# A new stored order for an attention and gated-MLP kernel: same instructions, other places and engines

## The chip, the cores and the metric

The kernel runs on one core of one Trainium2 chip. The metric is the device time of one execution in microseconds (us). PE is the matrix engine, DVE the vector engine, ACT the scalar engine, POOL the GpSimd engine, SP the sync engine, which here issues nearly all DMAs. Each of the five works through a queue of its own strictly in order and waits on semaphores where it needs another's result.

## The reference

Attention over 8 batches, 8 heads, 576 places, head size 64, with a bias that a small MLP makes from relative positions; its output goes through a gate (a causal convolution of 5 taps and a sigmoid), a product with w_val, and a product with w_out.

```python
scores = scale * np.matmul(q, k.transpose(0, 1, 3, 2))          # 8 x 8 x 576 x 576
x = (psi_rel / psi_i)[..., None]                                # log1p(|i-j|) / log1p(max(i,1))
bias = np.maximum(x @ w1 + b1, 0.0) @ w2                        # hidden 32, 8 heads
scores = scores + bias.transpose(2, 0, 1)[None]
attn = np.exp(scores - np.max(scores, axis=-1, keepdims=True))
attn = attn / (np.sum(attn, axis=-1, keepdims=True) + 1e-09)
x = np.matmul(attn, v)                                          # -> (8, 576, 512)
gate = sigmoid(sum_k conv_w[k] * shifted(x, k))                 # 5 taps
return gate * (x @ w_val) @ w_out
```

All is float32; the kernel splits the operands of the large products into a high and a low float16 part where it doesn't multiply in float32.

## The kernel before

**Start.** `bias_rows` makes the bias of 16 rows at a time: four `relu` tasks (L328 on ACT, L330 on DVE, or POOL), products on PE (L349), evictions (L368 on ACT, L370 on DVE), a store to DRAM by SP (L395). 36 such groups fill five tiles in DRAM, from which `load_bias` (L417, L420) loads the bias of a pair of heads, in the layout that the scores have.

**Attention.** `pair(n)` is one batch and two heads, 32 of them. SP loads its q and k (`qk_ld`, L610) into one of two `qk` buffers. Each pair has four blocks of 128 rows and half of a remainder block. A block is one QK product of 1.2 us on PE (L700, L716 for the remainder) into two `sp` tiles of PSUM, of which there are only two, so a block's two `logits` on DVE (L746: bias added, row maximum) must be over before the next QK product may start. Then come `expo` on ACT (L758), and one of two ways to transpose the weights. In 12 pairs ("T" in `TRANS`) the weights are normalised first (`norm`, L803) and PE transposes them (L848). In the other 20 they are split into float16 parts (`top`, L208 or L212 or L210; `rest`, L231, on POOL or DVE), and the DMA transposes them (`swap`, L882, L885, issued by SP). PE multiplies them with V (`piece`, L917) into a `po` tile, one of four PSUM tiles of the ring `ps`.

In the 20 pairs the sums are divided out afterwards, and here a `po` tile has two users beside the products: `ev` on ACT (L226) reads its first 256 columns, and `rb` on PE (L962) writes the broadcast reciprocals into its last 256, which `mu` on DVE (L972) reads. Neither needs the other's result, but they share the tile, and the one that comes later in the program waits for the one that comes first.

**MLP.** When a batch's four pairs are done, `mlp` makes its gate (convolution on DVE and ACT, L1097, L1106; tanh, L1118), the products `val` (L1172) and `outp` (L1227), and the stores. This work is spread between the QK products of later pairs.

**Preparation of weights.** `weight` takes each of nine weight pieces through six bit operations on DVE (`double_step`, L431 to L455) and a split. The absolute maximum of each V (`vmax`, L622, L635) is a DVE task too.

**What sets the order.** Every such step is a `Task` with the engines that may do it. `Plan.order` decodes a table, `ORDER`, of two bytes a task: the number of the task times four, plus which of its engines does it. The program is built in exactly that order; it gives each engine its queue, each tile its buffer from the ring, and decides which of two users of a tile comes first. Of 4115 tasks 1557 have more than one engine to choose from.

## Time and profile before

| | |
|---|---|
| median of 3 runs | 720.48 us (717.33 to 724.47) |
| the profiled execution | 725.42 us, its span 723.6 us |
| PE busy | 673.0 us |
| DVE busy | 639.4 us |
| ACT busy | 593.6 us |
| POOL busy | 446.5 us |
| granted TensorE clock, mean | 0.987 |

The page counts a matmul as busy from its start to its modelled end. A row of waits says which engine, line and tile waited, for what, and how long in total, how often, and at most. A row of the timeline is one instruction or a run of equal ones.

### The profile page before, as it was taken

How to read it: one execution, taken by the hardware profiler on the slowest of the kernel's cores; microseconds unless marked ns; L12 is line 12 of the kernel's file. 1: busy time of each engine (PE TensorE's matmuls, PEld its weight loads, DVE VectorE, ACT ScalarE, POOL GpSimd, SP SyncE). 2: the span in 40 equal slices, each digit the busy share in tenths (PEclk: the TensorE clock that was granted, in tenths of full speed). 3: DMA queues.
4: the chain of work that ended last, by engine and by line, in shares of the span. 5: the costliest groups of instructions: out<-in, count | busy, mean ns of one | idle time of the engine just before them, and what ended most of it. 6: DMA issues, size and time to landing. Idle time of an engine off the chain costs nothing. (4 is left out here: it accounts for less than half of the span.)

```text
span 723.6 us, 17323 instructions
## 1 busy us (share of the span) xinstructions
PE 673.0 (93%) x6144; PEld 421.0 (58%) x6144; DVE 639.4 (88%) x1656; ACT 593.6 (82%) x1323; POOL 446.5 (62%) x624
## 2 busy tenths in 40 slices
PE   6899899999999999888899999997999998998997
PEld 2225576666666755555567665564676665566754
DVE  7999799999998998997889898889889998888982
ACT  6999578988999987888668877798878898899761
POOL 0004455667788677667767778776658876766541
PEclk9999899999999999999999999998999999999999
DMA  5888972312299879999983589999953899899813
GB/s 161 262 311 294 318 234 63 125 67 62 70 158 180 193 171 199 220 222 185 175 184 97 127 176 199 202 210 199 190 125 99 181 209 189 177 201 202 150 45 116
DMA packets 263302, 125.73 MB, mean 174 GB/s; under 512 B 239792, under 2 KB 240048, under 8 KB 263216
## 3 DMA queue, kind: packets, MB, share of 16 engines
q1 hardware_dynamic: 263072, 124.34, 76.3%
q8 instruction: 48, 0.79, 0.5%
q10 hardware_dynamic: 144, 0.29, 0.1%
q14 instruction: 38, 0.31, 0.1%
HBM read 44.64 MB, written 20.33 MB: 90 GB/s over the span
## 5 line engine op out<-in xcount | busy, mean ns | idle before, releaser
L758 ACT ACTIVATE t_d<-t_d,nm 128x576 f32<-128x576 f32 x288 | 222.2, 774 | 45.1 <-DVE nm L746 39.4
L231 POOL TENSOR_TENSOR t_d<-t_d 128x512 f16<-128x512 f32 (+1 forms) x203 | 193.2, 969 | 71.6 <-ACT t_d L208 55.1
L746 DVE CUSTOM_DVE_ANT_0 t_d<-t_sp,bias 128x576 f32<-128x576 f32 x256 | 186.2, 749 | 25.2 <-PE t_sp L700 15.6
L700 PE MATMUL t_sp<-t_qk 64*128 64x288 f32 x1024 | 179.8, 433 | 9.9 <-DVE nm L746 7.4
L917 PE MATMUL t_ps<-t_pt,t_w 128*64 128x256 f16 (+1 forms) x1600 | 130.9, 309 | 8.1 <-DMA t_pt<-t_d 4.9
L700 PEld LDWEIGHTS t_sp<-t_qk 64*128 64x128 f32 x1024 | 101.6, 187 | 60.9 <-DVE nm L746 24.9
L803 POOL TENSOR_SCALAR t_d<-t_d,rinv 128x576 f32<-128x576 f32 x94 | 74.3, 801 | 43.6 <-DVE rinv L786 17.7
L208 ACT CAST t_d<-t_d 128x576 f16<-128x576 f32 x139 | 91.0, 667 | 8.0 <-DVE t_d L231 2.5
L1172 PEld LDWEIGHTS <-wv 128*128 128x128 f16 x768 | 72.7, 99 | 33.2 <-issue 11.9
L1172 PE MATMUL t_ps<-xh,wv 128*128 128x320 f16 (+1 forms) x512 | 75.9, 292 | 0.0
L848 PE MATMUL t_ps<-ident,t_d 128*128 128x128 f32 x486 | 69.9, 285 | 2.7 <-ACT t_pt L208 1.0
L917 PEld LDWEIGHTS <-t_w 128*64 128x64 f16 x1120 | 57.7, 110 | 25.2 <-issue 18.2
L848 PEld LDWEIGHTS t_ps<-ident,t_d 128*128 128x128 f32 x486 | 53.8, 143 | 25.9 <-issue 9.0
L1106 DVE SCALAR_TENSOR_TENSOR t_ps<-t_xp,convw,t_ps 128x288 f32<-128x288 f32 x126 | 65.2, 518 | 2.5 <-ACT t_ps L1097 0.3
L208 ACT COPY t_pt<-t_ps 128x512 f32<-128x512 f32 (+1 forms) x123 | 53.8, 480 | 11.3 <-PE t_ps L848 11.0
L1227 PE MATMUL t_ps<-wo,gh 128*128 128x512 f16 x256 | 61.7, 380 | 0.5 <-DVE gh L210 0.5
L758 ACT ACTIVATION_READ_ACCUMULATOR t_d<-t_d,nm 128x1 f32 x288 | 55.7, 194 | 0.0
L349 PE MATMUL t_ps<-rel,w 128*32 128x288 f32 (+17 forms) x352 | 46.1, 487 | 6.6 <-DVE rel L330 3.0
L231 DVE TENSOR_TENSOR t_d<-t_d 128x512 f16<-128x512 f32 (+1 forms) x67 | 48.5, 737 | 2.9 <-POOL t_d L212 1.5
L330 DVE TENSOR_SCALAR rel<-gt,sct,nb 128x576 f32<-128x576 f32 (+17 forms) x107 | 46.5, 500 | 0.0
L231 POOL TENSOR_TENSOR gl<-t_w,gh 128x256 f16<-128x256 f32 x42 | 29.3, 699 | 25.9 <-ACT gh L208 20.4
L917 PEld LDWEIGHTS t_ps<-t_pt,t_w 128*64 128x64 f32 x480 | 31.7, 137 | 23.1 <-issue 5.3
(139 smaller groups left out, 1078.8 us busy)
## 6 DMA issues: line engine op xcount, KB each, us to landing
t_qk<-qkd SPq DMA_DIRECT2D x32, 576.0 KB, 4.5
bias_d<-t_be SPq DMA_DIRECT2D x36, 295.5 KB, 6.0
bias<-bias_d SPq DMA_DIRECT2D x16, 576.0 KB, 7.1
out<-t_w SPq DMA_DIRECT2D x32, 256.0 KB, 2.6
t_w<-vd SPq DMA_DIRECT2D x20, 320.0 KB, 3.6
t_w<-vn SPq DMA_DIRECT2D x12, 320.0 KB, 3.7
t_d<-wvd SPq DMA_DIRECT2D x4, 512.0 KB, 5.1
t_d<-wod SPq DMA_DIRECT2D x4, 512.0 KB, 5.7
```

The lines of the kernel that those rows point to most:

```text
L208: A.copy(out=out, in_=in_)
L231: (V if e == "V" else G).tensor_tensor(out=out, in0=in0, in1=in1, op=ALU.subtract)
L330: (G if e == "G" else V).tensor_scalar(out=rel[g].t[:, 0:w], in0=src, scalar1=sct[:, mm : mm + 1], scalar2=nb1, op0=ALU.mult, op1=ALU.max,)
L700: T.matmul(ts[a][:, j, 0:hw], lhsT=qk.t[r, c * P : (c + 1) * P], rhs=qk.t[r, x : x + hw], start=True, stop=True,)
L746: V.tensor_tensor_reduce(out=part(c, a).rearrange("p (j f) -> p j f", j=2), in0=sp.t[:, :, 0 : S // 2], in1=bias.rearrange("p (j f) -> p j ...
L758: A.activation(out=part(c, a), in_=part(c, a), func=AF.Exp, bias=nms[c][:, a : a + 1], scale=-1.0, accum_out=sums[c][:, a, 0:1],)
L803: (G if e == "G" else V).tensor_scalar(out=t, in0=t, scalar1=rinvs[c][:, a : a + 1], scalar2=1.0, op0=ALU.mult, op1=ALU.mult,)
L848: T.transpose(t[:, k * P : (k + 1) * P], es[c].t[:, (k0 + k) * P : (k0 + k + 1) * P], ident)
L917: T.matmul(po.t[r, 0:256], lhsT=vt.t[:, v, r], rhs=pt[:, x, :, :] if tr else pt[:, :, x, :], start=(t == 0 and m == 0), stop=(t == 4 and m ...
L1106: V.scalar_tensor_tensor(out=o, in0=x, scalar=wt, in1=t, op0=ALU.mult, op1=ALU.add)
L1172: T.matmul(pm.t[:, 0:w], lhsT=weights["wv"][wi][:, k, d * P : (d + 1) * P], rhs=xb.t[xi][:, k, 0:w], start=(q == 0 and k == 0), stop=(q == ...
L1227: T.matmul(pm.t, lhsT=gb.t[gi][:, k, o : o + P] if o < 256 else gx.t[gi][:, k, :], rhs=weights["wo"][wi][:, k, :], start=(q == 0 and k == ...
```

## The change

Only `ORDER` is another. The tasks, what they depend on, the buffers and every other constant stand as before, and each engine's instructions come from the same tasks. 503 of the 1557 tasks with a choice go to another engine: 149 from DVE to POOL and 129 back, 71 from DVE to ACT and 63 back, 46 from POOL to ACT and 45 back. The number of PE instructions stays at 7637, and SP's at 286. In the new program the line numbers are lower by 2 than in the old one, as the table is two lines shorter: L700 becomes L698, L962 becomes L960.

The words that come with the change say that the table was searched for longer, with transfers taken to land later, and with the two users of a PSUM tile in sequence.

```diff
 BUFS = dict(w=13, d=6, pt=2, sp=2, ps=4, qk=2, rel=3, be=9, xp=2, xh=1, gh=1, gx=1)
 ORDER = (
-    'c-mE04`?Fyo}b+{W|EyGlQ?E4$s{`_lVr?Jl1VbzOp?jg9zL*#d$?c^d${0xxM0B^_OM_Nd)S8sd$?c^7cAJrJ>0_{?qR`qSg^%{3qG(9dswjG9`3^h7cAI^J?vrOzP~ZqzV{t}-{1H9`F_6N-'
...
+    'c-nPW0cav;n|60cGue!Bl8nhDnPex)BpJ<QGf5_!Nix}5u;35&a1RSE*ux$!_=7zxSg?l$d$@-M3+~~91s5#X!v+7t9`<m-9v1A6|6vac?qPo{Sg>Hhg8i{z!5;U1WA^WVaQEtb-'
...
 )
```

Three places show how queues change. The first is on PE, late in the program, at an `rb` (L962, later L960). The rows are PE's, with the semaphores that a row waits for; `wv` is w_val's float16 parts, `xl` the low part of the attention's output, `t_sp` the score tiles. Before:

```order
L1172 LDWEIGHTS wv_102
L1172 MATMUL t_ps<-xl,wv_102 128x320 [waits Pool_49]
L1172 LDWEIGHTS wv_102
L1172 MATMUL t_ps<-xl,wv_102 128x320
L962 MATMUL t_ps<-ident,rinvs 64x128 [waits Activation_49]
L962 MATMUL t_ps<-ident,rinvs 64x128 x3
L700 MATMUL t_sp<-t_qk 128x288 [waits DVE_49] x2
```

The same `rb` in the changed program; `t_pt` are transposed weights, `t_w` V:

```order
L915 LDWEIGHTS t_w
L915 MATMUL t_ps<-t_pt,t_w 64x256
L960 MATMUL t_ps<-ident,rinvs 64x128 x4
L698 MATMUL t_sp<-t_qk 128x288 [waits DMAHW6_49,DVE_49]
L698 MATMUL t_sp<-t_qk 128x288 [waits DVE_49]
L698 MATMUL t_sp<-t_qk 128x288 x2
```

The `rb` now follows its last `piece` at once and no longer waits for ACT: it stands ahead of `ev` in the table, so that `ev` waits for it. In the whole program ten rows of L962 wait for ACT before, and seven of L960 afterwards.

The second place is on PE too, where the program before has two QK products behind each other with nothing between (eight matmuls are two blocks); `gh` is the gated value's high part. Before:

```order
L1227 LDWEIGHTS gh
L1227 MATMUL t_ps<-wo_104,gh 128x512
L700 MATMUL t_sp<-t_qk 128x288 x8
L917 LDWEIGHTS t_w
L917 MATMUL t_ps<-t_pt,t_w 64x256
```

The first of these two QK blocks in the changed program:

```order
L1170 LDWEIGHTS wv_102
L1170 MATMUL t_ps<-xl,wv_102 128x320
L698 MATMUL t_sp<-t_qk 128x288 x4
L1170 LDWEIGHTS wv_102
L1170 MATMUL t_ps<-xh,wv_102 128x320
```

No two QK blocks stand together there any more: `val` products are on both sides.

The third is on DVE, in the start, among the `relu` rows (L330, later L328); `vcol` is V's maximum, `t_be` the bias rows, `t_w<-t_d` a step of the weight preparation. Before:

```order
L330 TENSOR_SCALAR rel<-gt,sct,nb_133 128x368 x3
L622 TENSOR_REDUCE vcol<-t_w 128x1
L330 TENSOR_SCALAR rel<-gt,sct,nb_133 128x336 x3
L330 TENSOR_SCALAR rel<-gt,sct,nb_133 128x352 x2
L370 TENSOR_SCALAR t_be<-t_ps,cadd 128x368
L330 TENSOR_SCALAR rel<-gt,sct,nb_133 128x352
L330 TENSOR_SCALAR rel<-gt,sct,nb_133 128x320 x3
L330 TENSOR_SCALAR rel<-gt,sct,nb_133 128x304
L622 TENSOR_REDUCE vcol<-t_w 128x1
```

The changed program at about the same rows:

```order
L328 TENSOR_SCALAR rel<-gt,sct,nb_133 128x400 x3
L328 TENSOR_SCALAR rel<-gt,sct,nb_133 128x384 x3
L429 TENSOR_SCALAR t_w<-t_d 128x512
L328 TENSOR_SCALAR rel<-gt,sct,nb_133 128x416 x3
L432 TENSOR_SCALAR t_w<-t_w 128x512
L328 TENSOR_SCALAR rel<-gt,sct,nb_133 128x352 x3
L328 TENSOR_SCALAR rel<-gt,sct,nb_133 128x368 x3
L328 TENSOR_SCALAR rel<-gt,sct,nb_133 128x304 x3
L435 TENSOR_SCALAR t_w<-t_w 128x512
```

Ahead of the last `relu` the old table has five `vmax`, seven `double_step` and four `logits` on DVE, the new one one, ten and six.

## The prediction

> **What bounds the kernel now.** I read the page's span and busy times first, then a table by stage, then the waits of PE, ACT and SP, and last single places in the timeline.

> ```profile
> span 723.6 us, 17323 instructions
> PE 673.0 (93%) x6144; PEld 421.0 (58%) x6144; DVE 639.4 (88%) x1656; ACT 593.6 (82%) x1323; POOL 446.5 (62%) x624
> 20.00:40.00 20.00, 17.59 (x131) 5.55 (x128) 19.97 (x51) 18.78 (x41) 1.43 (x1) 1.00 0.91 295
> 40.00:60.00 20.00, 18.51 (x132) 6.23 (x136) 20.00 (x50) 19.52 (x41) 0.00 (x0) 1.00 0.91 316
> 60.00:80.00 20.00, 15.01 (x118) 9.53 (x111) 16.83 (x48) 14.07 (x38) 10.16 (x13) 0.93 0.87 281
> 100.00:150.00 50.00, 49.24 (x431) 33.17 (x427) 48.69 (x142) 43.43 (x110) 32.27 (x47) 1.00 0.26 89
> 300.00:350.00 50.00, 43.63 (x461) 28.38 (x457) 44.18 (x110) 41.99 (x89) 36.22 (x43) 0.97 1.05 197
> 600.00:650.00 50.00, 46.33 (x433) 28.09 (x425) 43.26 (x107) 45.03 (x97) 33.61 (x44) 1.00 0.97 189
> 700.00:723.60 23.60, 19.17 (x105) 10.11 (x105) 8.55 (x18) 3.05 (x7) 6.16 (x13) 0.98 0.31 100
> ```

> The stages' columns are PE, its weight loads, DVE, ACT, POOL (busy us, instructions), granted clock, DMA share, GB/s. There are two regimes. From 20 to 60 us, while the bias is made, DVE has not 0.1 us free. From 100 us on PE is the busiest (49.24 of 50 us), but DVE follows closely (48.69), and in the loosest stretch PE has 6.4 us free (43.63 of 50). No PE instruction is added or removed, so the change can win only what PE, or DVE in the start, loses by waiting. If PE's busy time were its floor, that is 723.6 - 673.0 = 50.6 us at most.

> [...]

> What PE, ACT and SP wait for (total us, times, longest):

> ```profile
> PE t_sp L700 <- DVE nm L746: 7.4, 8, 3.4
> PE t_ps L962 <- ACT t_xp L226: 7.1, 5, 2.7
> PE t_ps L917 <- DMA t_pt<-t_d: 4.9, 6, 1.4
> PE t_ps L917 <- DMA t_w<-t_w: 2.5, 1, 2.5
> PE t_sp L700 <- DMA t_qk<-qkd: 2.0, 2, 1.3
> ACT t_xp L226 <- PE t_ps L962: 10.2, 9, 2.9
> SPq L610 <- PE t_sp L700: 51.4, 9, 12.0
> ```

> Two of the words that come with the change have a counterpart here: the two users of a PSUM tile (7.1 us of PE) and landings of DMAs (4.9 + 2.5 + 2.0 = 9.4 us).

> **The change part by part.** The sum is made against the profiled execution's 725.42 us, 0.7% above the median of 720.48; at the end the ratio is carried over to the median.

> *The two users of the tile.* The costliest case, PE's timeline (start, duration, wait in brackets):

> ```profile
> 602.89 1.25 PE L1172 MATMUL t_ps<-xh,wv 128*128 128x320 f16 x8
> 603.98 0.71 PE L1172 MATMUL t_ps<-xl,wv 128*128 128x320 f16 x4
> 607.42 0.66 PE L962 MATMUL t_ps<-ident,rinvs 128*64 128x128 f32 x8 [2.73 <-ACT t_xp L226]
> 608.01 1.24 PE L700 MATMUL t_sp<-t_qk 64*128 64x288 f32 x8
> ```

> This `rb` is the first place shown in the change: it waits 2.73 us for an ACT eviction whose result it doesn't need, and the QK product behind it waits too. Of the five `rb` that wait, four have lost their wait for ACT in the new table, this one among them; the fifth keeps it, but two `val` products now stand on PE in front. Seven rows still wait for ACT. If they cost nothing, 7.1 us go; if each costs the mean of the old ten (7.1 / 10 = 0.71), 7 x 0.71 = 5.0 stay and 2.1 go. By the table an `rb` comes after its `ev` 12 times before and 9 times afterwards; of the 12 six had no PE work at all between the two places, of the 9 one has none and the others 0.5 to 9 us. That is nearer to the first end. I take **-6.1 us**. What is late next: three more `ev` wait for `rb` instead (28 before, 31 now), at 10.2 / 28 = 0.36 us each, 1.1 us of ACT, which has 723.6 - 593.6 = 130 us free. I cost it at nothing; without that cover it is 1.1 us.

> *QK blocks that stand too close.* The second place of the change, in the trace of before:

> ```profile
> 282.76 1.95 PE L700 MATMUL t_sp<-t_qk 64*128 64x288 f32 x8
> 285.11 1.91 PE L700 MATMUL t_sp<-t_qk 64*128 64x288 f32 x8 [0.39 <-DVE nm L746]
> ```

> With nothing between them each block takes 0.7 us longer than the 1.24 us above, and 0.39 us of wait comes on top, because two score tiles must first be read by two `logits`. I added up the PE work that stands between one QK block and the next (taking, for instance, 1.25 / 2 us for four `val` matmuls as above), leaving out the start. Of 131 gaps 15 hold less than 1.5 us before, and 4 after; 5 hold more than 6 us before (the longest 10.7), and 1 after (6.6). Where a gap is long, DVE has no scores to read. So 11 places get rid of up to 0.7 us: -7.7 us at the most, and nothing if DVE, 88% busy, is late there anyhow. Between these ends I take about the middle, **-4 us**: the wait named after DVE above is 7.4 us in all, of which 3.4 us is a single one in the start.

> *The start.* DVE's prices there, and what moves between DVE and POOL (groups by shape):

> ```profile
> L622 DVE TENSOR_REDUCE vcol<-t_w 128x1 f32<-128x640 f32 x12 | 9.7, 809 | 0.0
> L437 DVE TENSOR_SCALAR t_w<-t_w 128x512 int32<-128x512 int32 (+1 forms) x9 | 3.7, 412 | 0.2
> L231 POOL TENSOR_TENSOR t_d<-t_d 128x512 f16<-128x512 f32 x132 | 158.3, 1206 | 69.6 <-ACT t_d L208 54.2 <-DVE t_w L1071 4.5 <-DVE t_d L210 3.6
> L231 DVE TENSOR_TENSOR t_d<-t_d 128x512 f16<-128x512 f32 x48 | 38.7, 809 | 2.9 <-POOL t_d L212 1.5 <-ACT t_d L208 1.1
> L231 POOL TENSOR_TENSOR gl<-t_w,gh 128x256 f16<-128x256 f32 x42 | 29.3, 699 | 25.9 <-ACT gh L208 20.4 <-ACT gxh L208 4.9 <-DVE gh L210 0.2
> ```

> Four `vmax` leave the full stretch of DVE (4 x 0.81 = 3.2 us) and three `double_step` enter it (3 x 0.41 = 1.2 us): 2.0 us less. The maxima return after 60 us, where DVE has 3.2 of 20 us free, so most of it holds. **-1.5 us**, between -3.2 and 0.

> *Subtractions that go to POOL.* Nine of 128x512 leave DVE: 9 x 0.809 = 7.3 us of DVE against 9 x 1.206 = 10.9 us of POOL, which has 277 us free. A single one is 0.4 us later on POOL. Were all nine on the path, that is +3.6 us; were DVE the bound throughout, -7.3. As neither is the busiest engine after 100 us I take **0**.

> [...]

> *Loads of q and k.* SP can issue such a load only when the buffer's old QK products are done, and PE's work from there to the first new QK product must cover the rest. The price is the landing, from issue, for L610:

> ```profile
> DMA to landing us min/median/max: 3.5/4.5/8.1
> ```

> Before, 4 of the 30 turns hold less than 7 us of PE work (4.8, 4.9, 6.2 and 6.3), and PE waited 2.0 us in two. Afterwards 8 do (five of 5.0 to 5.4, then 5.9, 6.6 and 6.7). Twice as many at the same price is **+2 us**. The lower end is 0; at the upper end all land after 8.1 us, a shortfall of 8 x 8.1 - 45.0 = 19.8 us against 4 x 8.1 - 22.2 = 10.2 before, so +9.6. The transposes by DMA (4.9 us) I leave as they are: the PE work between the place of a `swap` and its first `piece` has a median of 3.0 us before and 3.3 after.

> *The end.* Behind the last QK block PE's queue holds 4.5 us less work than before. PE's total is the same, so this is no term of its own.

> Sum: -6.1 - 4 - 1.5 + 0 + 2 = -9.6 us, 715.8 us for the profiled execution, a ratio of 0.987, and **711 us** for the median.

> **The rivals.** A measurement of this kernel tells a change of about 1% from none (713.3 to 727.7 us count as none; the three runs before lie 1% apart).

> *The waits move elsewhere.* DVE's load falls by 1% only, and a new order that frees PE of one wait meets another engine at 82 or 88%. Against it is that the waits named above had a direct cause in the order. With a net of -5 to +5 us the time is about 719.

> *The loads come late (slower).* Place: the first QK product of the pairs with the eight short turns; price: up to +9.6 us by themselves. SP must reach the load in its queue, in which L610 already stood up to 12.0 us behind PE's QK products, and the transposes stand behind it. It decides once SP is 2 us late on top of a landing of 4.5 us, since 5.0 to 5.4 us of cover are then gone: then each of the eight stalls PE by about 1.3 us, the longest of the two seen: 8 x 1.3 - 2.0 = +8.4 us. The transposes behind in SP's queue are late by as much, which doubles it, and half of the other gains is left: 720.5 + 16.8 - 5.8 = 731 us.

> [...]

> *A larger gain.* PE's busy time hides waits, as the 1.95 us show. If the QK gaps that are now even spare 0.15 us at each of 131 blocks, 20 us, twice the sum, go: 700 us.

> **How the numbers follow.** The forecast (-5 to -16 us) 0.50, of which 0.08 lies within 1%; the waits move 0.23; loads late 0.13; lock-out 0.04; larger gain 0.10. Faster by over 1%: 0.42 + 0.10 = 0.52. Within 1%: 0.08 + 0.21 + 0.04 = 0.33, and 0.02 of the moved waits with the late loads give 0.15 slower. The forecast's own range, 704 to 715, comes from the ends of its terms (-7.1 - 7.7 - 1.5 and -2.1 - 4 - 1.5 + 2). The range of all cases reaches to 725, which leaves out most of the late loads, and down to 700.

> **What would show it.** Right: the wait of L960 for ACT falls to about 1 us; L698 for DVE falls under 5 us; DVE at 20 to 60 us still full, but the first transposes on PE (L846) start 1 to 2 us earlier; PE's wait for t_qk at 4 us. Wrong: PE's busy time or its waits for t_qk, t_pt or DVE grow by more than these save. If L960's wait is gone and the time is the same, the waits have moved.

## The result and the profile after

The changed kernel takes 696.4 us (median of 4 runs, 692.2 to 698.7) against 720.7 us (the three runs of the table of before and one more): a ratio of 0.9655, 95% interval 0.9587 to 0.9722. Timed once more beside the experiments it gave 0.9616 (0.9581 to 0.9650). The forecast was 711 us, a ratio of 0.987, with a range of 700 to 725. The direction was right, the size was not, and the time fell below the range. The profiled execution took 698.68 us, its span is below.

Span, busy times and stages of the changed kernel, in the columns of the prediction:

```profile
span 696.2 us, 17319 instructions
PE 659.1 (95%) x6144; PEld 418.3 (60%) x6144; DVE 623.7 (90%) x1631; ACT 593.1 (85%) x1332; POOL 457.3 (66%) x637
20.00:40.00 20.00, 18.27 (x129) 5.57 (x126) 20.00 (x52) 19.51 (x43) 3.61 (x2) 1.00 0.99 337
40.00:60.00 20.00, 18.82 (x144) 6.78 (x147) 20.00 (x49) 18.90 (x42) 0.39 (x1) 1.00 0.96 313
60.00:80.00 20.00, 15.35 (x117) 8.76 (x110) 16.75 (x46) 14.12 (x36) 11.00 (x16) 0.91 0.87 280
100.00:150.00 50.00, 49.10 (x439) 33.87 (x440) 48.60 (x138) 44.26 (x112) 33.15 (x47) 1.00 0.41 138
300.00:350.00 50.00, 49.38 (x468) 31.57 (x470) 45.21 (x111) 43.92 (x97) 37.95 (x49) 1.00 0.96 187
600.00:650.00 50.00, 49.04 (x475) 30.64 (x474) 46.33 (x114) 46.55 (x100) 34.69 (x43) 1.00 1.01 187
```

The span is 27.4 us shorter. PE's idle time fell from 50.6 to 37.1 us, which is 13.5 us; the other 13.9 us left PE's *busy* time, with the very same 6144 products. DVE is busy for 15.7 us less, and only about half of this is work. Price each of its instructions undisturbed, at the duration that a tenth of its like stay under (same line and shape, in all 20 profiles of this case): they sum to 685 us before and 678 after (they overlap, so the sums are above the busy times). What they take beyond this price fell from 58 to 50 us, and most of that, 53 and 42 us, belongs to instructions that began while one of POOL's was running; the last section shows how. The loosest stretch of before (43.63 of 50 us from 300 to 350) is now nearly full, and the first 60 us look as they did.

PE's waits for the users of a PSUM tile, for scores and for transfers (total us, times, longest):

```profile
PE t_ps L960 <- ACT t_xp L224: 2.1, 2, 1.4
PE t_sp L698 <- DVE nm L744: 1.4, 4, 0.6
PE t_sp L698 <- DMA t_qk<-qkd: 1.7, 2, 1.1
PE t_ps L915 <- DMA t_w<-t_w: 4.3, 2, 2.8
PE t_ps L915 <- DMA t_w<-vn: 2.3, 1, 2.3
PE t_ps L915 <- DMA t_pt<-t_d: 0.4, 1, 0.4
```

`rb` (L960) waits 2.1 us instead of 7.1, and the scores cost 1.4 us instead of 7.4. The landings come to 8.7 us (1.7 + 4.3 + 2.3 + 0.4) against 9.4: other transfers are late now, but about as much in all.

What the waits leave out is seen in the weight loads of the QK product, which PE takes while the products before them still run: 1012 of the 1024 began so in the old kernel's trace and 1011 in the new one's, an exception to the strict order of the opening section. (Otherwise the lines of each engine begin in the program's order in the old trace, but for six fills on DVE that begin 10 to 66 ns after the instruction behind them.) The same group on the page of before, then of the changed kernel (busy us, mean ns | idle us before it, and the largest cause):

```profile
L700 PEld LDWEIGHTS t_sp<-t_qk 64*128 64x128 f32 x1024 | 101.6, 187 | 60.9 <-DVE nm L746 24.9
```

```profile
L698 PEld LDWEIGHTS t_sp<-t_qk 64*128 64x128 f32 x1024 | 97.8, 186 | 52.2 <-DVE nm L744 15.8
```

They wait for DVE's `logits` for 15.8 us instead of 24.9. By the two traces 7.4 and, after the change, 1.8 us of these waits are idle time of PE. For 8.5 us in either PE was still at earlier products, which costs nothing. The other 9.0 and 5.5 us lie inside QK blocks and count as PE busy: the first two of a block's eight matmul rows run while its second `sp` tile is still being read, and the third waits (0.42 and 0.38 us in the blocks at 282.76 and 285.11 us of the old trace).

### The profile page after: what moved, and what is told of

Its sections match the earlier page's. It is cut to its first block, busy times and chain, and to the rows that moved or that the text cites. A ratio compares the mean times of both kernels' runs of the same rounds, so it can differ in the third digit from the quotient of the medians.

```text
span 696.2 us, 17319 instructions
## 1 busy us (share of the span) xinstructions
PE 659.1 (95%) x6144; PEld 418.3 (60%) x6144; DVE 623.7 (90%) x1631; ACT 593.1 (85%) x1332; POOL 457.3 (66%) x637
## 5 line engine op out<-in xcount | busy, mean ns | idle before, releaser
L229 POOL TENSOR_TENSOR t_d<-t_d 128x512 f16<-128x512 f32 (+1 forms) x211 | 202.6, 977 | 64.9 <-ACT t_d L206 41.8
L698 PE MATMUL t_sp<-t_qk 64*128 64x288 f32 x1024 | 172.4, 430 | 3.5 <-DMA t_qk<-qkd 1.7
L698 PEld LDWEIGHTS t_sp<-t_qk 64*128 64x128 f32 x1024 | 97.8, 186 | 52.2 <-DVE nm L744 15.8
L801 POOL TENSOR_SCALAR t_d<-t_d,rinv 128x576 f32<-128x576 f32 x94 | 75.0, 809 | 45.9 <-DVE rinv L784 35.2
L206 ACT CAST t_d<-t_d 128x576 f16<-128x576 f32 x145 | 94.2, 667 | 8.7 <-DMA t_pt<-t_d 3.0
L1170 PE MATMUL t_ps<-xh,wv 128*128 128x320 f16 (+1 forms) x512 | 74.3, 286 | 2.3 <-DVE t_w L213 1.2
L915 PEld LDWEIGHTS <-t_w 128*64 128x64 f16 x1120 | 58.3, 111 | 21.0 <-issue 15.6
L846 PE MATMUL t_ps<-ident,t_d 128*128 128x128 f32 x486 | 67.0, 280 | 3.8 <-POOL t_d L801 2.3
L846 PEld LDWEIGHTS t_ps<-ident,t_d 128*128 128x128 f32 x486 | 52.7, 141 | 24.5 <-POOL t_d L801 8.8
L915 PEld LDWEIGHTS t_ps<-t_pt,t_w 128*64 128x64 f32 x480 | 33.7, 137 | 24.1 <-issue 4.8
L328 DVE TENSOR_SCALAR rel<-gt,sct,nb 128x576 f32<-128x576 f32 (+17 forms) x106 | 47.0, 512 | 0.1
L229 DVE TENSOR_TENSOR t_d<-t_d 128x512 f16<-128x512 f32 (+1 forms) x59 | 41.9, 719 | 3.0 <-ACT t_d L206 2.6
L1225 PEld LDWEIGHTS <-gh 128*128 128x128 f16 x256 | 23.1, 98 | 32.6 <-issue 6.9
```

The costliest lines, as they stand in the source:

```text
L206: A.copy(out=out, in_=in_)
L229: (V if e == "V" else G).tensor_tensor(out=out, in0=in0, in1=in1, op=ALU.subtract)
L328: (G if e == "G" else V).tensor_scalar(out=rel[g].t[:, 0:w], in0=src, scalar1=sct[:, mm : mm + 1], scalar2=nb1, op0=ALU.mult, op1=ALU.max,)
L698: T.matmul(ts[a][:, j, 0:hw], lhsT=qk.t[r, c * P : (c + 1) * P], rhs=qk.t[r, x : x + hw], start=True, stop=True,)
L801: (G if e == "G" else V).tensor_scalar(out=t, in0=t, scalar1=rinvs[c][:, a : a + 1], scalar2=1.0, op0=ALU.mult, op1=ALU.mult,)
L846: T.transpose(t[:, k * P : (k + 1) * P], es[c].t[:, (k0 + k) * P : (k0 + k + 1) * P], ident)
```

## The experiments

Each kernel was timed beside the old one on the same chip. Differences in us are the ratio times 723 us, the median of the old kernel there (722.9 to 723.8); times inside one trace are from the start of the span. The tables can't be read as text, so each edit of a table is written as a rule on the list of (task, engine), and "old" and "new" are the two tables.

### Where along the run does the gain arise?

Both tables hold the same tasks, and at most places only some ten of them stand on the two sides of a cut. So the first part of one table can be followed by the rest of the other.

```diff
-table = old
+table = new[:722]  + [x for x in old if x.task not in new[:722]]    # 19 QK blocks
+table = old[:722]  + [x for x in new if x.task not in old[:722]]    # the reverse
+table = new[:1914] + [x for x in old if x.task not in new[:1914]]   # 64 QK blocks
+table = new[:2393] + [x for x in old if x.task not in new[:2393]]   # 84 QK blocks
```

New up to the 19th block:

> The new table up to its 19th QK block, the old order from there on; what is computed stays. Theory: the start alone brings what the two traces show there, the 19th QK block 6.5 us earlier, so about 714 us against 720.5 (ratio 0.991), and with it the PE idle time of 3.4 us at 75 us and the 6.8 us of half clock behind it become shorter. Rival, the forecast's size of this term (1.5 us): 719 us, 0.998. Rival, the parts only work together: 720.5, 1.000.

Measured: 722.4 us, ratio 0.9996 (0.9964 to 1.0027). The start brings nothing. The theory falls here, and with it the way it was read: it took the n-th QK block as a measure of progress. The start of the QK block that has so many others ahead of it (us):

```
ahead      12     24     40     64     84    130
old      103.1  148.5  206.4  323.9  413.0  616.1
new       95.0  141.1  201.7  318.3  397.1  585.1
start_new 94.6  145.9  203.8  322.3  411.4  613.8
```

The kernel with the new start has the whole lead of 8.5 us behind 12 blocks, and 2.6 us behind 40. A view by stage of that kernel shows what takes it back:

```profile
100.00:150.00 50.00, 48.45 (x423) 32.31 (x423) 48.04 (x135) 43.80 (x110) 32.66 (x47) 1.00 0.38 126
150.00:200.00 50.00, 48.78 (x399) 32.62 (x400) 48.12 (x132) 45.43 (x109) 35.71 (x45) 1.00 0.23 74
```

DVE is busy for 96 of the 100 us there, PE for 97. A QK block that comes earlier leaves other work behind it, and in these stretches neither engine has room to catch up. That the lead was such a loan is argued from these rows; that it ends in no gain is measured.

Old up to the 19th block, new from there on:

> The reverse: the old table up to its 19th QK block, then the new one; what is computed stays. Theory: the new table less its start, 696.4 + 6.5 = 703 us (ratio 0.976). Rival, a start of 1.5 us: 698 us (0.968). Rival, the parts only work together: 710 us or more.

Measured: 695.3 us, 0.9587 (0.9545 to 0.9629). The new kernel itself, once more:

> The new kernel unchanged, timed beside the three kernels below. Expected as before: ratio 0.966 (0.959 to 0.972). With the old start it was 0.959; if the new start costs something, as the splices suggest, this one is again above 0.963; if the two are the same, about 0.960.

Measured: 694.7 us, 0.9616 (0.9581 to 0.9650). The two aren't told apart, which agrees with a start that is worth nothing.

> The new table up to its 64th QK block, the old order from there on. Theory: between the 19th and the 64th block the traces gain nothing (6.5 and 5.6 us earlier), so about 715 us, the same as with the new start alone (ratio 0.992). Rival, the gain is spread evenly over the QK blocks by closer spacing: 720.5 - 6.5 - 18 x 45/124 = 707.5 us (0.982).

Measured: 719.8 us, 0.9938 (0.9909 to 0.9967). This is near the theory's 0.992, whose reason, 6.5 us from the start, had fallen.

> The new table up to its 84th QK block, the old order from there on. Theory: the stretch from the 64th to the 84th block holds two long waits of PE before (2.51 and 2.05 us) and 3.4 us of half clock, and the traces gain 10.4 us in it: 715 - 10.4 = 704.5 us (0.978). Rival, an even gain: 707.5 - 18 x 20/124 = 704.6 as well, but from 707.5, so the step from the kernel above is then only 2.9 us.

Measured: 710.4 us, 0.9797 (0.9753 to 0.9840). So the four stretches bring 0.3, 4.2, 10.2 and (to the 0.9616 of the whole) 13.1 us: 0, 0.09, 0.51 and 0.22 us a QK block. The stretch from 64 to 84 came out at the 10.4 us expected. Nearly all of the gain arises behind the 64th block, and it is not even.

### The forecast's two largest terms alone

The two users of the tile, in the old table:

```diff
 for rb in (10 of the 12 that stand behind their ev):
-    ..., ev, ..., rb, ...
+    ..., rb, ev, ...
```

> The old table with one thing changed: in 10 of the 12 places where an rb stood behind its ev, it now stands ahead of it, the five that waited 7.1 us among them; engines and all else stay, and so does what is computed. Forecast's term: -6.1 us (714.5; ratio 0.991). Theory after the splices: the 7.1 us go, 714 us (0.990), and no half clock with them, since none followed these waits. Rival: the ev that now waits, or the next user of the pair, takes the time back: 720.5 (1.000).

Measured: 716.2 us, 0.9892 (0.9855 to 0.9928), that is -7.8 us (-10.5 to -5.2). PE's waits in that kernel:

```profile
PE t_sp L698 <- DVE nm L744: 5.9, 10, 1.5
PE t_ps L915 <- DMA t_pt<-t_d: 5.1, 7, 1.3
```

The wait of L960 for ACT isn't among PE's waits any more, and these two, the next in size, stand about where they stood (7.4 and 4.9). Forecast and theory hold, the rival falls.

QK blocks at a distance, in the old table:

```diff
 for 17 PE tasks (val, outp, piece, tp) near two QK blocks that stand close:
-    qk, qk, task        or    task, qk, qk
+    qk, task, qk
```

> The old table with 17 PE tasks (val, outp, piece, tp) moved by a few places, so that the PE work that lacks to 1.5 us between QK blocks falls from 7.1 to 1.2 us in sum (15 gaps below 1.5 us before, 9 after, none below 1.25; the new table has four, 0.44 us the shortest); engines and computation stay. Forecast's term: -4 us, bounds 0 and -7.7 (716.5; 0.994). Theory after the splices: the gain sits at a few long waits, not in these gaps: -1 us (0.999). Rival: spacing is the main cause: -13 us (0.982).

Measured: 726.5 us, 1.0072 (1.0046 to 1.0097), slower by 5.2 us. Of that kernel:

```profile
span 725.0 us, 17327 instructions
PE 672.1 (93%) x6144; PEld 418.5 (58%) x6144; DVE 639.1 (88%) x1656; ACT 592.4 (82%) x1323; POOL 447.5 (62%) x624
PE t_ps L915 <- DMA t_pt<-t_d: 7.5, 7, 3.3
PE t_sp L698 <- DVE nm L744: 6.6, 9, 1.9
```

PE still waits 6.6 us for the scores, and the wait of `piece` for its transposes rose from 4.9 to 7.5 us, with a single one of 3.3. Room between the blocks, made for itself, moves the waits. None of the three expectations had the sign. The test is not a clean one: the 17 tasks themselves came earlier or later by it, and by the expectation nine gaps under 1.5 us were left, where the new table has four.

### Order or engines?

```diff
-table = old
+table = [(task, engine of task in new) for task in old]     # old order, new engines
+table = [(task, engine of task in old) for task in new]     # new order, old engines
```

> The old order, but each of the 503 tasks that the new table gives to another engine runs on that engine; computation stays. DVE gets 28 tasks less, ACT 9 and POOL 19 more. Forecast: 0 (720.5; 1.000). Theory: the choice of engines fits the order it was found with, so here nothing or a loss: 720 to 730 us (1.000 to 1.013). Rival: DVE's 15.7 us less of busy time are the main cause of the gain: 710 us or less (0.985).

Measured: 793.8 us, 1.0984 (1.0940 to 1.1028).

> The new order with the old engines for the 503 tasks; computation stays. Forecast: as the new kernel, 696.4 us against 720.5 (ratio 0.966). Theory: the order alone keeps the places of the long waits apart but loses their fit with the engines: 702 to 712 us (0.974 to 0.988). Rival: the engines are the main cause: 711 us or more.

Measured: 786.1 us, 1.0880 (1.0830 to 1.0929). Either half of the change alone costs 64 to 71 us, far more than any theory said, and both together bring 28. The old order with the new engines (busy times, two waits, span and mean clock):

```profile
PE 697.1 (88%) x6144; PEld 430.8 (55%) x6144; DVE 638.1 (81%) x1631; ACT 598.8 (76%) x1332; POOL 457.3 (58%) x637
PE t_sp L698 <- DVE nm L744: 21.7, 26, 2.7
PE t_ps L960 <- ACT t_xp L224: 9.9, 5, 4.7
core 0: 789.3 us, clock 0.970
```

No engine is above 88%, so none is overloaded: it is waiting that grew, for scores from 7.4 to 21.7 us, and with it the time at half clock (mean clock 0.970 against 0.987). DVE has the tasks of the new kernel here and is busy for 638.1 us all the same, where that has 623.7: its instructions take 61 us beyond their undisturbed price instead of 50. A task's place in the table is where its own engine was due to be free. On another engine that place is too early or too late, and whatever stands behind it in that queue waits along. This reading is argued; measured is that neither half does without the other.

To see if a few such moves are free, as the forecast had costed nine of them, only the subtractions were moved back:

```diff
-table = new
+table = [(task, engine in old if task is rest or rest8 else engine) for (task, engine) in new]
```

> The new order and engines, but the 96 subtractions rest and rest8 that the new table moved between DVE and POOL (52 to POOL, 44 to DVE) run where they ran before; what is computed stays. The forecast costed such moves at 0 (ratio 0.962). Theory after the runs with all engines exchanged (+64 and +71 us for 503 tasks): a subtraction stands in the table where its own engine is free, so it costs in proportion, 96/503 x 92 = 17 us (0.986). Rival: all the loss came from a few other kinds of task: at most 3 us (0.966).

Measured: 714.9 us, 0.9884 (0.9851 to 0.9918): 19.4 us slower than the new kernel, near the 17 of the theory. DVE's load and two waits in that kernel, then the same two waits in the new one:

```profile
PE 667.4 (94%) x6144; PEld 422.1 (59%) x6144; DVE 629.8 (89%) x1639; ACT 594.5 (84%) x1332; POOL 450.2 (63%) x629
POOL t_d L229 <- ACT t_d L206: 51.1, 41, 4.0
ACT t_d L756 <- DVE nm L744: 42.1, 49, 2.3
```

```profile
POOL t_d L229 <- ACT t_d L206: 41.8, 44, 3.2
ACT t_d L756 <- DVE nm L744: 30.0, 39, 2.0
```

POOL waits 51.1 us for a `top` where it waited 41.8 in the new kernel, and ACT waits 42.1 us for scores where it waited 30.0.

### What a microsecond of DVE is worth

Four kernels with another load on DVE. A first trial, a fill of 16 columns behind each of the 288 `logits`:

```diff
                     V.tensor_tensor_reduce(... accum_out=nms[c][:, a : a + 1])      # logits
+                    V.memset(dum, 0.0)                                              # 128x16
```

> [...] Theory: DVE's smaller load is what lets scores be read in time, and brings 8.8 us of PE's busy time and the 6 us of its waits for DVE; so +8 to +15 us against the new kernel (ratio 0.977 to 0.987). Rival: the load of DVE is covered, it is the fit of the order that counts: at most +3 us (0.970).

Measured: 695.1 us, 0.9614 (0.9582 to 0.9645), the same as the new kernel. But the page shows that this was no load:

```profile
PE 657.3 (95%) x6144; PEld 416.7 (60%) x6144; DVE 623.8 (90%) x1919; ACT 593.7 (86%) x1332; POOL 457.5 (66%) x637
L753 DVE MEMSET dum<- 128x16 f32 x288 | 20.7, 72 | 0.0
```

288 fills of 72 ns are there, and DVE's busy time is still 623.8 us: 20.4 of their 20.7 us lie inside the records of their neighbours. The run decides nothing on DVE's load. With a heavier instruction, and from the other side:

```diff
                     V.scalar_tensor_tensor(out=o, in0=x, scalar=wt, in1=t, ...)     # taps 1 to 4
+                    if tp < 4: V.tensor_scalar(out=cb.t[:, 288:328], in0=x[:, 0:40], scalar1=wt, ...)
```

```diff
-                    V.scalar_tensor_tensor(out=o, in0=x, scalar=wt, in1=t, ...)     # taps 1 to 4
+                    V.scalar_tensor_tensor(out=o[:, 0:w], in0=x[:, 0:w], in1=t[:, 0:w], ...)  # w = 168 if tp < 4 else 288
```

> The new kernel with one more DVE instruction behind each of the taps 1 to 3 on half rows: 126 scalings of 40 columns into a part of the PSUM bank that nobody reads; by the rows for 1 column (0.147 us) and 288 columns (0.514 us) some 0.2 us each, of which about 0.13 lies outside their neighbours' records: 16 us more of DVE. What is computed stays. Theory, by the kernel with lighter taps (13.0 us less of DVE brought 0.5%, 3.7 us): +4 to +5 us (ratio 0.968 against 0.962). Rival, DVE's load is the main cause: +10 us or more (0.976). Rival, it is covered: 0.962.

> The old kernel with part of the gate's convolution left out: of the taps 1 to 3 on half rows (126 of the 168 instructions of L1106, 0.518 us each for 288 columns) only the first 168 columns are computed, 126 x 120 columns x about 1.04 ns = 15.7 us less of DVE; order and engines stay. Theory: the time falls by 8 to 15 us (706 to 713 us against 720.5, ratio 0.979 to 0.989). Rival, the load of DVE is covered: 718 to 721 us (0.997 or more).

> The old kernel with the same 126 scalings of 40 columns behind the taps, 33.1 us more of DVE by the new kernel's row (0.263 us each); what is computed stays. If DVE's time counts the same in both tables, 0.72 x 33.1 = +24 us (ratio 1.033). If the old table has more slack around DVE because its PE waits elsewhere, as its 3.7 us for 13 us suggest, 0.28 x 33.1 = +9 us (1.013).

> The new kernel with the same part of the convolution left out as in the old one before (taps 1 to 3 on half rows: 168 of 288 columns), 13 us less of DVE. If DVE's time counts in the new table whatever the direction, -0.72 x 13 = -9 us against the new kernel (ratio 0.949). If taking away brings little because PE, ACT and the order bound it then, -3.7 us (0.957) or less.

Measured: the new kernel with load 0.9949 (0.9927 to 0.9971), the old one with load 1.0364 (1.0315 to 1.0412), the old one lightened 0.9948 (0.9919 to 0.9978), the new one lightened 0.9569 (0.9532 to 0.9606). Busy times in that order:

```profile
PE 671.4 (93%) x6144; PEld 422.8 (59%) x6144; DVE 656.3 (91%) x1757; ACT 595.0 (83%) x1332; POOL 457.2 (64%) x637
```

```profile
PE 686.2 (91%) x6144; PEld 427.2 (57%) x6144; DVE 674.6 (90%) x1782; ACT 594.2 (79%) x1323; POOL 450.8 (60%) x624
```

```profile
PE 668.2 (93%) x6144; PEld 417.7 (58%) x6144; DVE 626.4 (88%) x1656; ACT 593.3 (83%) x1323; POOL 446.7 (62%) x624
```

```profile
PE 656.8 (95%) x6144; PEld 417.4 (60%) x6144; DVE 608.1 (88%) x1631; ACT 592.7 (86%) x1332; POOL 458.8 (66%) x637
```

The lightened taps of 168 columns take 392 ns in the old kernel where those of 288 took 518, which is 1.05 ns a column. Added, a microsecond of DVE costs 24.1 / 32.6 = 0.74 us in the new kernel and 26.3 / 35.2 = 0.75 in the old one. Taken away, it brings 3.8 / 13.0 = 0.29 in the old one and 3.4 / 15.6 = 0.22 in the new one (where the interval reaches to nothing). Of the expectations the higher prices were right, or still too low, for load that is added, and the lower ones, nearly, for load that is taken away. It is the direction that matters and not the table. A reading that no run tests: an engine at 90% has little room for more work, while work taken out leaves a hole that the fixed order behind it fills only in part.

### Do long waits and the clock add up?

In the old kernel's trace a long idle time of PE is followed by half the clock. Its stages at 498 us (the third column from the end is the granted clock):

```profile
498.00:500.00 2.00, 0.00 (x0) 0.00 (x0) 1.04 (x4) 1.64 (x4) 1.71 (x2) 1.00 1.28 154
501.00:502.00 1.00, 1.00 (x10) 0.54 (x10) 0.91 (x5) 0.97 (x5) 0.00 (x0) 0.50 1.06 133
506.00:507.00 1.00, 1.00 (x6) 0.56 (x4) 0.75 (x1) 0.14 (x1) 1.00 (x2) 0.50 0.02 3
508.00:509.00 1.00, 1.00 (x10) 0.57 (x7) 0.20 (x1) 0.10 (x1) 1.00 (x2) 1.00 1.06 205
```

PE idles 2.4 us and then runs at 0.50 for 6.8 us. Three such places make 17.1 us at half clock in the old kernel; the new one has two, 6.8 us. In full-clock work that is 5.1 us of the 13.9 us that PE's busy time lost. These are two single executions. Over the 88 of the old kernel beside the experiments the time lost to the clock, (1 - clock) times the execution, has a mean of 5.8 us, over the ten of the new kernel 2.3; and among the 88 a microsecond lost so goes with 0.8 us of the whole (straight line through them, standard error 0.08). So the clock's part of the gain is some 3 us, by estimate. To test it, work was added to the new kernel inside its idle places:

```diff
 def piece(...):      # t == 0 of three pairs only, 6, 7 and 4 times
+    T.matmul(po.t[:, 256:384], lhsT=ident, rhs=ident, start=True, stop=True)
```

> The new kernel with 17 extra matmuls of 128x128 (ident by ident, into columns that rb overwrites later), 6, 7 and 4 of them ahead of the first piece of three pairs, where PE stood 2.31, 2.81 and 1.52 us; what is computed stays. Each such matmul takes some 0.28 us by the L846 row, so 4.8 us of work are added inside 6.6 us of idle time. Theory: a stretch of 3.4 us in which PE is busy for too little of it halves the clock of the next one; the added work keeps PE above that, the two half-clock stretches at 71 and 297 us are gone from the records, and the time falls by up to 3.4 us (ratio about 0.004 under the kernel above). Rival 1: the clock doesn't depend on it, the time is the same. Rival 2: the matmuls delay what follows, +1 to +5 us.

Measured: 692.2 us, 0.9575 (0.9542 to 0.9608). Of the changed kernel, then of this one:

```profile
280.00:300.00 20.00, 17.19 (x212) 12.23 (x210) 17.89 (x50) 15.47 (x36) 13.69 (x19) 0.92 1.13 223
core 0: 696.2 us, clock 0.995
```

```profile
280.00:300.00 20.00, 19.76 (x227) 13.32 (x226) 18.29 (x49) 17.35 (x40) 15.57 (x21) 1.00 1.17 213
core 0: 689.4 us, clock 1.000
```

With 17 products more, the clock stays at 1.000 in this execution. In the four others it was 0.996 to 0.999, against 0.993 to 0.999 in the six of the new kernel beside it. The time is 2.5 us lower in the median (690.7 to 693.2 us against 693.0 to 696.6), but the intervals of the two ratios overlap (0.9581 to 0.9650 for the new kernel). So the clock is raised and not full, and the gain in time isn't quite shown.

Next, only the long waits were taken out of the old kernel:

```diff
 table = old with the ten rb first
-    ..., qkr, ..., val, ...                      # the qkr at 498 us
+    ..., val, qkr, ...
 def piece(...):      # t == 0 of the pair at 330 us, 6 times
+    T.matmul(po.t[:, 256:384], lhsT=ident, rhs=ident, start=True, stop=True)
```

> The old table and its engines with three places mended: the ten rb ahead of their ev as before, one val product moved ahead of the qkr that waited 2.42 us at 498 us, and 6 extra matmuls of 128x128 ahead of the piece that waited 2.51 us at 330 us, so that the clock stays up. What is computed stays. Theory, these waits and the half clock behind them add up: 7.8 us (measured) + 1.2 to 2.4 + 3.4 of half clock at 501 us + 1.7 of half clock at 333 us = some 14 us: 709 us (ratio 0.980). Rival, the waits move on: no more than rb alone, 715 us (0.989).

Measured: 714.6 us, 0.9892 (0.9852 to 0.9931), no better than `rb` alone. Its mean clock and its wait for scores:

```profile
core 0: 717.6 us, clock 0.997
PE t_sp L698 <- DVE nm L744: 8.4, 15, 2.1
```

The half clock went from 17.1 us to 3.4 us, and the wait for scores from 7.4 to 8.4 us. The theory falls: outside of `rb`, the old order doesn't keep what a mended place brings.

Last, the new kernel with both mends:

```diff
 new kernel with the 17 products, and
-    ..., ev, ..., rb, ...       # five places
+    ..., rb, ev, ...
```

> The new kernel with the 17 extra matmuls of the earlier run and five more rb ahead of their ev (at most two PE tasks are passed); what is computed stays. Theory: ratio 0.9575 with the matmuls alone, less the 1.8 us that L960 still waited for ACT: 0.955, faster than the old and the new kernel. Rival: those rb weren't on the path: 0.9575.

Measured: 694.0 us, 0.9593 (0.9561 to 0.9626). This, the old start with the new rest (0.9587) and the 17 products alone (0.9575) are all lower than the new kernel's 0.9616, and their intervals all overlap its own. None is shown to beat it.

### The waits inside the QK blocks

From the traces I took each QK block after 90 us, away from half clock: the time from its first product to PE's next task, less 1.15 us, about the median; and whether the second `logits` of the block before ended only after it had begun (a few ns decide one or two of these counts).

```
kernel                        excess us, sum   blocks begun with scores unread
old                                30.8           45 of 133
old, rb first                      32.2           48
old, spread                        28.2           37 of 130
old, lighter taps on DVE           30.2           43
new, old engines for rest          27.0           44 of 131
new                                20.3           31
new, again                         18.6           32 of 132
old start, new rest                20.7           32
old, DVE loaded                    40.7           54 of 129
new, DVE loaded                    30.2           44 of 132
new, lighter taps on DVE           16.8           22
```

Here are 10 us of the gain that the table of waits doesn't show. Neither room between blocks nor a lighter DVE alone moves the old 30 us much. Load on DVE does: it adds 10 us in either kernel, of the 24 and 26 us that it costs in all. The new table's `logits` come on time more often, and giving 96 tasks their old engine undoes two thirds of that; that it is the fit of order and engines which does it is argued from these rows.

## Why the prediction was wrong

**The two users of the tile (-6.1 us): right.** Done alone, -7.8 us (-10.5 to -5.2).

**QK blocks that stand too close (-4 us, bounds 0 and -7.7): too small, and wrong in its cause.** The step was that a place with less than 1.5 us of PE work costs 0.7 us and is rid of it by room. Room took 2.6 us off the blocks of the old kernel (28.2 against 30.8), and the whole became 5.2 us slower. In the new kernel the blocks lost 10 us, and PE's wait for scores another 6.0 (of which some 3 belong to one wait of 3.4 us in the start). What else moves them that much, by the runs, is DVE's load and not the distance.

**The start (-1.5 us): small, and smaller still.** -0.3 us (-2.6 to +2.0). The first transposes of PE do start 2.1 us earlier (62.9 against 65.0 us), as the prediction said; it leads to nothing. The sum also left out that the new table has two `logits` more in that stretch (six against four, 0.75 us each), so hardly 0.5 of its 2.0 us was saved.

**Subtractions that go to POOL (0, bounds -7.3 and +3.6): the step that failed.** It read: "As neither is the busiest engine after 100 us I take 0". Yet every QK block needs DVE's reading of the one before, busiest engine or not: a microsecond more of DVE costs 0.75 us of the whole in either kernel, and one less brings 0.29 in the old one. DVE's busy time fell by 15.7 us and not by 7.3, which by these prices is worth between 15.7 x 0.29 = 4.6 and 15.7 x 0.75 = 11.8 us (an estimate). Its second error was to count nine moves out of 503. The price of a move isn't the difference of two durations: in the new table 96 subtractions on their old engines cost 19.4 us, beyond both bounds.

**Loads of q and k (+2 us): wrong, by its size.** Eight short turns cost the same 1.7 us that four cost before (2.0).

**The rivals.** The larger gain, 700 us with a chance of 0.10, was nearest, and its sentence that PE's busy time hides waits was right: it fell by 13.9 us with the same products. Its mechanism, even gaps, is not shown to have done it. That the waits move elsewhere is what befell the mended and the spread old kernels, not the new one. Loads that come late fell. That DVE and POOL lock each other out had a chance of 0.04: it was the author's estimate, and that it makes the kernel slower no run shows. What the trace of before shows is DVE held by POOL (last section): 89 of DVE's instructions took 43 us beyond their undisturbed price. The prediction's row of the 48 subtractions on DVE, 809 ns, is a mean in which held ones (up to 1.64 us) and undisturbed ones (0.68 to 0.69 us) are mixed. With nine more subtractions on POOL it costs DVE less and not more, as fewer are held in the new order (78): 50 us beyond the undisturbed price against 58. What these 8 us are worth by themselves no run shows.

**What the sum left out** is the clock. The rows with a clock of 0.93 and 0.97 stood in the prediction, and no term was made of them; 5.1 us by the records of the two profiles, some 3 us over all executions. The two places left in the new kernel brought 2.5 us in the median when they were filled.

**The forecast's own range**, 704 to 715, was also narrower than its terms: at its slow end it took the QK blocks at -4 and the start at -1.5 us, whose bounds were 0.

Shown by a run of its own is thus 7.8 us (`rb`). The 4.6 to 11.8 us for DVE's load and the 3 us for the clock are estimates, and the former lie partly in the same place as the 10 and 6 us of the scores, so they are not to be added up. What the rest is made of stays open beyond this: it arises after the 19th block, most of it after the 64th, it needs order and engines together, and it shows as scores that are read in time.

## What to carry to other kernels

Where order and engines come from one search, price the table as a whole: half of it can cost more (64 to 71 us here) than the whole brings (28), so a sum over single edits says little. Read a second engine at 88 to 90% as part of the bound, and test it by adding work: here a microsecond added cost 0.74 to 0.75 us, and one taken away brought 0.22 to 0.29. Split a row by what ran beside it before you call an effect absent: its mean can mix two kinds of instruction (here 0.68 us undisturbed and up to 1.64 held, 809 ns in the mean). A lead at one milestone is no gain until the stretch behind it has room to keep it.

## What the runs showed of the hardware

```
matmul time in 3.41 us   steps   followed by half clock
under 1.25                  20          20
1.25 to 1.5                 16          14
1.5 to 2.0                  61          23
2.0 to 2.25                 48           4
over 2.25                 3875           0
```

In these runs no fully idle step was needed: all 20 steps with under 1.25 us of matmuls and 14 of the 16 with 1.25 to 1.5 us were followed by half clock, and none of the 3875 with over 2.25 us. Up to the last matmul of a run, the emptiest of the 61 steps that were followed by it held 0.59 us of matmuls, and the longest gap within any of them was 2.8 us; in the old kernel's trace the one that begins at 497.19 us held 1.00 us, with a gap of 2.42 us. A wait of 2.7 us that was split between two steps (the `rb` at 605 us in the old kernel, 1.68 us of work left in the first) went free, as 38 of the 61 steps of its row do, and the one of 2.4 us in one step (498 us) was followed by 6.8 us of half clock. Where the steps fall differs from one execution to the next: they begin 2.26 us after the start of the span and then every 3.413 us in the old kernel's trace, 3.11 us after it in the new one's. So the same wait need not have the same price: of the new kernel's two profiles one has half clock at 71 and 297 us, the other at 457 us.

**Small DVE instructions can be free.** 288 fills of 16 columns, 72 ns each, changed neither DVE's busy time (623.8 us) nor the kernel's (0.9614 against 0.9616); 126 scalings of 40 columns into PSUM took 0.263 us each and cost 0.19 us each of the whole.

```profile
L1104 DVE TENSOR_SCALAR t_ps<-t_xp,convw 128x40 f32<-128x40 f32 x126 | 33.1, 263 | 4.5
```

**POOL can hold DVE up.** Two rows of the trace of before, one on each engine:

```profile
304.71 1.99 POOL L231 TENSOR_TENSOR t_d<-t_d 128x512 f16<-128x512 f32 x2 [1.58 <-ACT t_d L208]
304.90 1.51 DVE L231 TENSOR_TENSOR t_d<-t_d 128x512 f16<-128x512 f32 x1
```

There are 48 such subtractions on DVE. The 16 that met no instruction of POOL took 0.68 to 0.69 us. Fifteen that began under one of POOL's ended 0.54 to 0.55 us after that one's end, and took 0.74 to 1.64 us; three that began under a product with a scalar (L215, 1 or 256 columns) took 0.68 to 0.71 us and were not held. `logits`, which read the scores from PSUM, take 0.75 us with POOL beside them (243 of the 288) or without (45). In all, 89 instructions of DVE took over 0.15 us more than their undisturbed price before, 43 us together, and each of the 89 began under an instruction of POOL; after the change they are 78, with 35 us.
